# Expert blocks of two sizes, the last ones behind a branch

## The chip, the cores and the metric

One core of one Trainium2 chip runs the whole program. The metric is the device time of an execution in microseconds. Five engines work side by side, each through its own list of instructions: TensorE (PE in the profile, with its weight loads apart as PEld), VectorE (DVE), ScalarE (ACT), GpSimd (POOL) and SyncE (SP), which here only issues transfers. PE writes to PSUM; DVE and ACT copy from there to SBUF.

## What is computed

A sliding-window attention over 8 batches of 576 tokens with 8 heads of 64, and then a mixture of 8 experts. A token goes through one expert: the one of its own largest logit, or the one of the token before it.

```python
logits = np.einsum('bsd,de->bse', x, w_gate)                # x: attention's output, D = 512
local_gate = 1.0 / (1.0 + np.exp(-np.einsum('bsd,de->bse', x, w_local).squeeze(-1)))
for b in range(B):
    prev_e = -1
    for s in range(S):
        fresh_e = int(np.argmax(logits[b, s]))
        if s == 0 or local_gate[b, s] < 0.5:
            e = fresh_e
        else:
            e = prev_e if prev_e >= 0 else fresh_e
        prev_e = e
        ...                                                  # p: softmax of logits[b, s]
        h = np.maximum(x[b, s] @ w1[e], 0.0)                 # w1[e]: 512 x 1024
        out[b, s] = p[e] * (h @ w2[e])                       # w2[e]: 1024 x 512
```

All is float32. There are N = 4608 tokens.

## The kernel before

The program has three stages, each written as a function. A scheduler puts the instructions of each engine in order; it keeps their dependences and knows the buffers of each pool, and may pull an instruction ahead of others.

`attention` (lines 76 to 226) goes through 36 chunks of 128 tokens: scores (L127), a masked softmax (L137 to L149), the values' product (L177, L181), rows of x to DRAM (`xs`, L192), and the logits (L204).

`route` finds each token's expert and its place. Each expert's tokens take whole blocks of 256 places, so there are at most NBLK = 25 blocks, in NS = 50 slots of 128 places. `cnt` is the count of tokens of each expert, `ends` where its blocks end, `pl` and `plc` the place of each token, `ej` the expert of each block. A loop of 36 steps (L389 to L395) turns places around into `idx`, the token of each place, and `pw`, its gate's value. Places that stay empty hold the token N, whose row of `xs` is zero, and which the scatter leaves out.

`experts` runs a fixed number of blocks. For each, `fetch` reads the block's expert into a register of SP, gathers two slots of rows by indirect transfers on POOL (`xg`, L418), and loads that expert's `w1` and `w2`, 2 MB each, from SP's queue (L424). `turn` transposes the rows on PE (`tp`, L432; copied to `xt` by DVE). `hidden` is 8 groups of 4 matmuls into `hp` (L440) with 128 by 128 tiles of `w1` as weights and 256 columns of `xt` streaming; DVE and ACT take turns to evict with a relu (L443, L445). `result` runs, for each slot, 8 matmuls of 512 columns into `yp` (L452), an eviction scaled by the gate's value (L455), and an indirect scatter on POOL (L456). The loop fetches and turns a block ahead of the one it computes. Weights have two buffers for each of `w1` and `w2`, gathered rows four.

Of the kernel before, what the change touches and what calls it, by code (L numbers as in the profile page):

```python
# [8 lines left out]
F32 = mybir.dt.float32  # L9
I32 = mybir.dt.int32  # L10
# [8 lines left out]
P = 128  # L19
# [16 lines left out]
NS = NBLK * BC  # L36
NEG = -1.0e9


@with_exitstack  # L40
def kernel(
    ctx: ExitStack,
    tc: tile.TileContext,
    q: bass.AP,
    k: bass.AP,
    v: bass.AP,
    wg: bass.AP,
    w1: bass.AP,
    w2: bass.AP,
    out: bass.AP,  # L50
):
# [9 lines left out]
    ej = const.tile([1, NBLK], I32, name="ej")  # L61
# [12 lines left out]

@with_exitstack
def attention(ctx, tc, q, k, v, xs, lt, wgs, ident):
    """Softmax over the window for each chunk of 128 tokens, then its rows of x and its logits.

    q and k have two heads on the partitions. The keys of a chunk are its own and the 64 before it.
    Within a tile of four heads, slot 2 * j + i is head 4 * half + 2 * i + j.  # L80
    """
    nc = tc.nc
# [6 lines left out]

    # A query p of a chunk sees the keys p < j <= p + 64 of the 192.  # L90
    masks = []
# [61 lines left out]
    def values(st, half):  # L153
# [76 lines left out]
def route(ctx, tc, lt, idx, pw, ej, ident):  # L230
    """The expert of each token, and the tokens in order of their experts.

    Each expert's tokens take whole blocks of BLK places. Place 128 * n + p is at [p, n] in idx (the token)
    and pw (its gate's value); places that stay empty have the token N.
    """
    nc = tc.nc
# [116 lines left out]
    nb_i = tl("nb_i", P, E, dt=I32)  # L353
    nc.vector.tensor_scalar(nb_i, cnt, float(BLK - 1), None, Alu.add)
    nc.vector.tensor_scalar(nb_i, nb_i, BLK.bit_length() - 1, None, Alu.arith_shift_right)
    nb = tl("nb", P, E)
    nc.vector.tensor_copy(nb, nb_i)
    ends = tl("ends", P, E)
    nc.vector.tensor_tensor_scan(ends, nb, zero[:, :E], 0.0, Alu.add, Alu.add)
    off = tl("off", P, E)  # L360
    nc.vector.tensor_tensor(off, ends, nb, op=Alu.subtract)
    nc.vector.scalar_tensor_tensor(off, off, float(BLK), base[:, :, 0], Alu.mult, Alu.subtract)
    nc.vector.tensor_tensor(base, base, over(last(off), [P, E, C]), op=Alu.add)
    pl = tl("pl", *CE)
    nc.vector.tensor_tensor(pl, pre.rearrange("p (c e) -> p c e", e=E), base.rearrange("p e c -> p c e"), op=Alu.add)
    nc.vector.tensor_tensor(pl, pl, oh, op=Alu.mult)
# [11 lines left out]

    # The expert of block n: how many experts end at or before it.
    ec = tl("ec", 1, NBLK, E)  # L380
    nc.vector.tensor_tensor(ec, over(iob, [1, NBLK, E]),
                            over(ends[0:1, :].rearrange("p (o e) -> p o e", o=1), [1, NBLK, E]), op=Alu.is_ge)
    ef = tl("ef", 1, NBLK)
    nc.vector.tensor_reduce(ef, ec, axis=AX.X, op=Alu.add)
    nc.vector.tensor_scalar(ej, ef, float(E - 1), None, Alu.min)
# [15 lines left out]
def experts(ctx, tc, xs, w1, w2, out, idx, pw, ej, ident):  # L401
    """Each block's tokens through its expert: rows of x gathered, rows of the output scattered."""
    nc = tc.nc
    wp = ctx.enter_context(tc.tile_pool(name="ex_w", bufs=2))
    xp = ctx.enter_context(tc.tile_pool(name="ex_x", bufs=2 * BC))
    wk = ctx.enter_context(tc.tile_pool(name="ex_work", bufs=2))
    ps_t = ctx.enter_context(tc.tile_pool(name="ex_ps_t", bufs=2, space=PSUM))
    ps_h = ctx.enter_context(tc.tile_pool(name="ex_ps_h", bufs=3, space=PSUM))
    ps_y = ctx.enter_context(tc.tile_pool(name="ex_ps_y", bufs=2, space=PSUM))

    def fetch(n):
        st = {}
        e = nc.values_load(ej[0:1, n:n + 1], engines=[ET.SP], min_val=0, max_val=E - 1,
                           skip_runtime_bounds_check_because="a count of experts, at most E - 1")
        st["x"] = []
        for i in range(BC):
            x = xp.tile([P, D], F32, name="xg")
            nc.gpsimd.indirect_dma_start(  # L418
                out=x, out_offset=None, in_=xs[:, :],
                in_offset=bass.IndirectOffsetOnAxis(ap=idx[:, n * BC + i:n * BC + i + 1], axis=0))  # L420
            st["x"].append(x)
# [5 lines left out]
    def turn(st):  # L427
        st["xt"] = xt = wk.tile([P, DK, BLK], F32, name="xt")
        for i in range(BC):
            tp = ps_t.tile([P, DK, P], F32, name="tp")  # L430
            for kk in range(DK):
                nc.tensor.transpose(tp[:, kk, :], st["x"][i][:, kk * P:(kk + 1) * P], ident)  # L432
            nc.vector.tensor_copy(xt[:, :, i * P:(i + 1) * P], tp)

    def hidden(st):
        st["h"] = h = wk.tile([P, FK, BLK], F32, name="h")
        for m in range(FK):
            hp = ps_h.tile([P, BLK], F32, name="hp")
            for kk in range(DK):
                nc.tensor.matmul(hp, lhsT=st["w1"][:, kk, m * P:(m + 1) * P], rhs=st["xt"][:, kk, :],  # L440
                                 start=(kk == 0), stop=(kk == DK - 1))
            if m % 2:
                nc.vector.tensor_relu(h[:, m, :], hp)  # L443
            else:
                nc.scalar.activation(h[:, m, :], hp, Act.Relu)  # L445

    def result(st, n):
        for i in range(BC):
            s = n * BC + i
            yp = ps_y.tile([P, D], F32, name="yp")  # L450
            for m in range(FK):
# [6 lines left out]
                in_=y, in_offset=None, bounds_check=N - 1, oob_is_err=False)  # L458

    st = fetch(0)  # L460
    turn(st)
    for n in range(NBLK):
        nxt = fetch(n + 1) if n + 1 < NBLK else None
        hidden(st)
        if nxt:
            turn(nxt)
        result(st, n)
        st = nxt


# [29 lines left out]
```

## Time and profile before

| | |
|---|---|
| time, median of 3 runs | 1394.6 us (1388.53 to 1434.29) |
| span of the profiled execution | 1410.9 us (the profile has no other time of it) |
| PE busy | 1360.3 us, 96% |
| PEld busy | 1001.3 us, 71% |
| DVE, ACT, POOL busy | 332.0, 261.5, 134.5 us |
| first hidden layer starts | 694.80 us |
| DMA | 166.04 MB; q1 (SP's transfers) 133.17 MB, q0 (POOL's) 32.02 MB |

A row of the profile's groups names line, engine and operation, then what is written and read, the shape, the count, the busy time and the mean length of one in ns, and after the bar the idle time before them and what ended it. A row of the timeline starts with the start and the length of a merged run of instructions in us; PE's runs end with the last matmul's drain, so that neighbours overlap by some tenths. A row of the stretches has, after its bounds and length, the busy time (and number) of PE, PEld, DVE, ACT and POOL, then PE's granted clock, DMA's busy share and GB/s. Every float32 matmul leaves two records on PE and two on PEld; a transposition leaves one. The clock digits in the strip of slices are tenths of the full clock.

### The profile page before, as it was taken

What the parts mean: (1) busy time and instruction counts of PE and PEld (TensorE: products, weight loads), DVE (VectorE), ACT (ScalarE), POOL (GpSimd) and SP (SyncE); (2) the same over time, 40 slices, a digit from 0 to 9 for tenths busy, and PEclk for the clock granted to TensorE, in tenths of its full rate; (3) what the DMA queues carried; (4) which work ended last, traced back from release to release, by engine and by line L of the source; (5) the groups of instructions that cost most, each with busy time, mean ns of one, the idle gap of its engine ahead of it and who ended that gap; (6) DMA issues with size and microseconds to landing.
All of it is one profiled execution on the core that took longest, in us unless ns stands there. A gap on an engine that the chain in (4) does not pass through costs nothing. (4 is left out here: it accounts for less than half of the span.)

```text
span 1410.9 us, 13404 instructions
## 1 busy us (share of the span) xinstructions
PE 1360.3 (96%) x5322; PEld 1001.3 (71%) x5322; DVE 332.0 (24%) x688; ACT 261.5 (19%) x828; POOL 134.5 (10%) x222
## 2 busy tenths in 40 slices
PE   7999999999999999976499999999999999999998
PEld 5888788887888788865366677667766776667665
DVE  3533333233333334348110011001110011001100
ACT  3432332232232234220011111111101110111011
POOL 1000000000000000000201111111111111111100
PEclk7855555555555557555599999999999999999999
DMA  9202300033000000000745454545354545454520
GB/s 348 85 15 105 127 15 16 8 105 127 15 15 15 16 15 24 15 16 20 293 143 200 156 202 147 217 157 215 141 217 157 208 151 208 166 186 172 192 74 0
DMA packets 35678, 166.04 MB, mean 118 GB/s; under 512 B 4493, under 2 KB 16797, under 8 KB 29216
## 3 DMA queue, kind: packets, MB, share of 16 engines
q1 hardware_dynamic: 24672, 133.17, 25.8%
q0 software_dynamic: 10944, 32.02, 5.9%
q8 instruction: 42, 0.69, 0.2%
q14 instruction: 20, 0.16, 0.0%
HBM read 146.29 MB, written 22.55 MB: 120 GB/s over the span
## 5 line engine op out<-in xcount | busy, mean ns | idle before, releaser
L440 PE MATMUL hp<-xt,w 128*128 128x256 f32 x1600 | 352.0, 381 | 0.0
L452 PE MATMUL yp<-w,h 128*128 128x512 f32 x800 | 347.5, 592 | 0.0
L440 PEld LDWEIGHTS hp<-xt,w 128*128 128x128 f32 x1600 | 305.9, 191 | 52.2 <-issue 11.5
L452 PEld LDWEIGHTS yp<-w,h 128*128 128x128 f32 x800 | 150.3, 190 | 179.5 <-issue 179.4
L443 DVE TENSOR_SCALAR h<-hp 128x256 f32<-128x256 f32 x100 | 42.5, 425 | 631.0 <-issue 360.7
L127 PE MATMUL sp<-kt,qt 64*128 64x192 f32 (+1 forms) x576 | 179.6, 553 | 8.2 <-DMA kt<-in_k_dram 8.0
L177 PEld LDWEIGHTS xo<-vt,owns 128*128 128x128 f32 x576 | 120.7, 310 | 23.8 <-issue 21.3
L127 PEld LDWEIGHTS sp<-kt,qt 64*128 64x128 f32 x576 | 100.1, 297 | 50.7 <-issue 45.5
L149 ACT ACTIVATE e<-s,nmax 128x192 f32<-128x192 f32 (+1 forms) x288 | 125.5, 438 | 41.9 <-DVE nmax L141 41.4
L177 PE MATMUL xo<-vt,owns 128*128 128x64 f32 x576 | 131.3, 404 | 0.0
L181 PE MATMUL xo<-vt,befs 64*128 64x64 f32 x512 | 116.7, 402 | 0.0
L181 PEld LDWEIGHTS xo<-vt,befs 64*128 64x128 f32 x512 | 109.2, 309 | 7.0 <-issue 3.5
L455 ACT ACTIVATE y<-yp,pw 128x512 f32<-128x512 f32 x50 | 34.4, 687 | 380.2 <-PE yp L452 380.2
L445 ACT ACTIVATE h<-hp 128x256 f32<-128x256 f32 x100 | 38.3, 383 | 325.1 <-PE hp L440 325.1
L161 PE MATMUL own<-ident,e 128*128 128x128 f32 x288 | 90.7, 418 | 0.0
L137 DVE SCALAR_TENSOR_TENSOR s<-sp,mask 128x768 f32<-128x768 f32 x64 | 61.0, 954 | 124.4 <-PE sp L127 124.2
L170 ACT COPY befs<-bef 64x512 f32<-64x512 f32 x64 | 37.1, 580 | 275.0 <-PE bef L168 274.9
L456 POOL DMA_INDIRECT out_dram<-y,idx x50 | 50.4, 1009 | 366.2 <-ACT y L455 358.9
L163 DVE COPY owns<-own 128x512 f32<-128x512 f32 x72 | 49.7, 691 | 124.9 <-PE own L161 123.2
L418 POOL DMA_INDIRECT xg<-xs,idx x50 | 48.7, 973 | 318.2 <-PE tp L432 268.0
L168 PE MATMUL bef<-ident,e 128*128 128x128 f32 x256 | 75.7, 409 | 0.0
L161 PEld LDWEIGHTS own<-ident,e 128*128 128x128 f32 x288 | 54.5, 214 | 27.0 <-issue 17.0
(118 smaller groups left out, 647.6 us busy)
## 6 DMA issues: line engine op xcount, KB each, us to landing
w<-in_w_dram SPq DMA_DIRECT2D x50, 2048.0 KB, 8.8
qt<-in_q_dram SPq DMA_DIRECT2D x12, 768.0 KB, 9.1
kt<-in_k_dram SPq DMA_DIRECT2D x12, 768.0 KB, 10.5
vt<-in_v_dram SPq DMA_DIRECT2D x12, 768.0 KB, 11.6
xs<-x POOLq DMA_DIRECT2D x36, 256.0 KB, 2.3
xg<-xs,idx POOLq DMA_INDIRECT x50, 8.1
out_dram<-y,idx POOLq DMA_INDIRECT x50, 2.8
wgs<-in_wg_dram POOLq DMA_DIRECT2D x1, 18.0 KB, 4.5
```

The source lines that it names most:

```text
L127: nc.tensor.matmul(sp[:, j, i * KW + lo:(i + 1) * KW], lhsT=qt[h, 2 * half + i, t0:t0 + P], rhs=kt[h, 2 * half + i, t0 - WIN + lo:t0 + P], ...
L137: nc.vector.scalar_tensor_tensor(s.rearrange("p j i k -> p j (i k)"), sp[:, :, :2 * KW], DH ** -0.5, m.rearrange("p (o x) -> p o x", o=1). ...
L149: nc.scalar.activation(e[:, o + lo:o + KW], s[:, j, i, lo:], Act.Exp, bias=nmax[:, j, i:i + 1], accum_out=st["sum"][:, h:h + 1])
L161: nc.tensor.transpose(own[:, s, :], e[:, o:o + P], ident)
L163: nc.vector.tensor_copy(owns, own)
L168: nc.tensor.transpose(bef[:, s, :], e[:, s * KW:s * KW + P], ident)
L177: nc.tensor.matmul(st["xo"][:, head(s)], lhsT=owns[:, s, :], rhs=vt[:, c, head(s)], start=(half == 0 and s == 0), stop=bool(st["lo"]), ski ...
L181: nc.tensor.matmul(st["xo"][:, head(s)], lhsT=befs[WIN:, s, :], rhs=vt[WIN:, c - 1, head(s)], start=False, stop=True, skip_group_check=True)
L418: nc.gpsimd.indirect_dma_start(out=x, out_offset=None, in_=xs[:, :], in_offset=bass.IndirectOffsetOnAxis(ap=idx[:, n * BC + i:n * BC + i + ...
L440: nc.tensor.matmul(hp, lhsT=st["w1"][:, kk, m * P:(m + 1) * P], rhs=st["xt"][:, kk, :], start=(kk == 0), stop=(kk == DK - 1))
L452: nc.tensor.matmul(yp, lhsT=st["h"][:, m, i * P:(i + 1) * P], rhs=st["w2"][:, m, :], start=(m == 0), stop=(m == FK - 1))
L456: nc.gpsimd.indirect_dma_start(out=out[:, :], out_offset=bass.IndirectOffsetOnAxis(ap=idx[:, s:s + 1], axis=0), in_=y, in_offset=None, bou ...
```

## The change

An expert's tokens go first into complete blocks of 256, and what is left into blocks of 128. Of complete blocks there are at least NB = 11 whatever the counts are, and exactly the first 11, in the order of experts, are used; tokens beyond these, and all remainders, go to at most NSM = 21 blocks of 128. Eighteen of these (SURE) always run; the last three run only if more than 18 are in use. Their rows and weights are fetched ahead of the branch in either case. There are now 43 slots.

```diff
-BLK = 256
-BC = BLK // P
-NBLK = (N + E * (BLK - 1)) // BLK
-NS = NBLK * BC
+BIG = 2 * P
+NB = -(-(N - E * (BIG - 1)) // BIG)
+SM0 = NB * 2
+SMALL = N - NB * BIG
+NSM = (SMALL + E * (P - 1)) // P
+SURE = SMALL // P + E // 2
+NBLK = NB + NSM
+NS = SM0 + NSM
```

The places: `nb` is the number of an expert's big blocks after the cap at 11, `ns` of its small ones, `lim` the tokens in its big blocks, `rank` a token's number within its expert.

```diff
+    nc.vector.tensor_scalar(bend, bend, float(NB), None, Alu.min)
+    nc.vector.tensor_scalar(boff, boff, float(NB), None, Alu.min)
+    nc.vector.tensor_tensor(nb, bend, boff, op=Alu.subtract)
...
+    nc.vector.tensor_tensor_scan(send, ns, zero[:, :E], 0.0, Alu.add, Alu.add)
...
     pl = tl("pl", *CE)
-    nc.vector.tensor_tensor(pl, pre.rearrange("p (c e) -> p c e", e=E), base.rearrange("p e c -> p c e"), op=Alu.add)
+    nc.vector.tensor_tensor(pl, rank, over(mid(lim), CE), op=Alu.is_ge)
+    nc.vector.tensor_tensor(pl, pl, over(mid(step), CE), op=Alu.mult)
+    nc.vector.tensor_tensor(pl, pl, rank, op=Alu.add)
+    nc.vector.tensor_tensor(pl, pl, over(mid(off), CE), op=Alu.add)
     nc.vector.tensor_tensor(pl, pl, oh, op=Alu.mult)
...
+    nc.vector.tensor_copy(ej[:, NBLK:], send[0:1, E - 1:])
```

The expert stage: buffers, the hidden layer in groups of 512 columns of PSUM (two tiles of 256 or four of 128), and the branch.

```diff
-    wp = ctx.enter_context(tc.tile_pool(name="ex_w", bufs=2))
-    xp = ctx.enter_context(tc.tile_pool(name="ex_x", bufs=2 * BC))
+    wp = ctx.enter_context(tc.tile_pool(name="ex_w", bufs=4))
+    xp = ctx.enter_context(tc.tile_pool(name="ex_x", bufs=6))
...
-        for m in range(FK):
-            hp = ps_h.tile([P, BLK], F32, name="hp")
-            for kk in range(DK):
-                nc.tensor.matmul(hp, lhsT=st["w1"][:, kk, m * P:(m + 1) * P], rhs=st["xt"][:, kk, :],
-                                 start=(kk == 0), stop=(kk == DK - 1))
-            if m % 2:
-                nc.vector.tensor_relu(h[:, m, :], hp)
+        each = 512 // n
+        for g in range(FK // each):
+            hp = ps_h.tile([P, each, n], F32, name="hp")
+            for i in range(each):
+                m = g * each + i
+                for kk in range(DK):
+                    nc.tensor.matmul(hp[:, i, :], lhsT=st["w1"][:, kk, m * P:(m + 1) * P], rhs=st["xt"][:, kk, :n],
+                                     start=(kk == 0), stop=(kk == DK - 1))
+            o = h[:, g * each:(g + 1) * each, :n]
+            if g % 2:
+                nc.vector.tensor_relu(o, hp)
...
+    sure = NB + SURE
     st = fetch(0)
     turn(st)
-    for n in range(NBLK):
-        nxt = fetch(n + 1) if n + 1 < NBLK else None
+    for n in range(sure):
+        nxt = fetch(n + 1) if n + 1 < sure else None
...
+    rest = [fetch(n) for n in range(sure, NBLK)]
+    used = nc.values_load(ej[0:1, NBLK:NBLK + 1], min_val=0, max_val=NSM,
+                          skip_runtime_bounds_check_because="a count of blocks, at most NSM")
+    with tc.If(used > SURE):
+        for st in rest:
+            turn(st)
+            hidden(st)
+            result(st)
```

PE's list, at the end of the expert stage. Before, its last three blocks (`w_` tiles are buffers of `w1` under `hp` and of `w2` under `yp`):

```order
L440 MATMUL hp<-xt,w_6031 128x256 x32
L432 MATMUL tp<-ident,xg 128x128 x8
L452 MATMUL yp<-w_6033,h 128x512 x16
L440 MATMUL hp<-xt,w_6132 128x256 x32
L432 MATMUL tp<-ident,xg 128x128 x8
L452 MATMUL yp<-w_6134,h 128x512 x16
L440 MATMUL hp<-xt,w_6233 128x256 x32
L452 MATMUL yp<-w_6235,h 128x512 x16
L496 UNCONDITIONAL_BRANCH
```

The same place now, with the last two of the 18 small blocks that always run, and what stands behind the branch up to its first block:

```order
L487 MATMUL hp<-xt,w_5957 128x128 x32
L475 MATMUL tp<-ident,xg 128x128 x4
L499 MATMUL yp<-w_5959,h 128x512 x8
L487 MATMUL hp<-xt,w_6024 128x128 x32
L499 MATMUL yp<-w_6026,h 128x512 x8
L518 TENSOR_LOAD ej
L520 COMPARE_AND_BRANCH
L475 MATMUL tp<-ident,xg 128x128 x8
L487 MATMUL hp<-xt,w_6142 128x128 x32
L499 MATMUL yp<-w_6144,h 128x512 x8
```

A small block keeps the 32 matmuls of the hidden layer, with half the columns, and has half the transpositions and half the result matmuls of a big one; the next block's transpositions still stand between hidden layer and result.

DVE's list in `route`, between the count of tokens `cnt` and the sum `plc`, where PE has nothing to do. Before:

```order
L352 TENSOR_TENSOR cnt<-run,base 128x8
L354 TENSOR_SCALAR nb_i<-cnt 128x8
L355 TENSOR_SCALAR nb_i<-nb_i 128x8
L357 CAST nb<-nb_i 128x8
L359 SCALAR_TENSOR_TENSOR ends<-nb,zero 128x8
L361 TENSOR_TENSOR off<-ends,nb 128x8
L381 TENSOR_TENSOR ec<-iob,ends 1x200
L362 SCALAR_TENSOR_TENSOR off<-off,base 128x8
L384 TENSOR_REDUCE ef<-ec 1x25
L363 TENSOR_TENSOR base<-base,off 128x288
L385 TENSOR_SCALAR ej<-ef 1x25
L365 TENSOR_TENSOR pl<-pre,base 128x288
```

Now, the part of it from the small blocks' ends (`send`) on:

```order
L382 SCALAR_TENSOR_TENSOR send<-ns,zero 128x8
L384 TENSOR_TENSOR soff<-send,ns 128x8
L421 TENSOR_TENSOR ec<-iob,send 1x168
L389 SCALAR_TENSOR_TENSOR step<-soff,off 128x8
L426 CAST ej<-send 1x1
L424 TENSOR_REDUCE ef<-ec 1x32
L390 SCALAR_TENSOR_TENSOR step<-step,lim 128x8
L402 TENSOR_TENSOR pl<-pl,step 128x288
L425 TENSOR_SCALAR ej<-ef 1x32
L403 TENSOR_TENSOR pl<-pl,rank 128x288
L404 TENSOR_TENSOR pl<-pl,off 128x288
L405 TENSOR_TENSOR pl<-pl,oh 128x288
```

Counted over the whole stretch, instructions of 128x8 go from 7 to 20, and element-wise ones of 128x288 from 3 to 7; those for the blocks' experts (`ec`, `ef`, `ej`) are interleaved with the chain in both.

POOL's list at the start of the expert stage, as a piece of the difference: gathers (`xg`) and scatters (`out_dram`).

```order
+L461 DMA xg<-xs,idx 128x512 x12
+L503 DMA out_dram<-y,idx 4608x512 x4
+L461 DMA xg<-xs,idx 128x512 x2
+L503 DMA out_dram<-y,idx 4608x512 x2
+L461 DMA xg<-xs,idx 128x512 x2
```

Before, ten gathers stand in the place of the twelve, and the rest of this piece is the same; in the small blocks one gather alternates with one scatter. The attention's part of every engine's list is unchanged.

More of the change, by code (lines that the diff above doesn't have):

```diff
@@ L60 @@
     pw = const.tile([P, NS], F32, name="pw")
-    ej = const.tile([1, NBLK], I32, name="ej")
+    ej = const.tile([1, NBLK + 1], I32, name="ej")
     ident = const.tile([P, P], F32, name="ident")
@@ L353, in route @@
     nb_i = tl("nb_i", P, E, dt=I32)
-    nc.vector.tensor_scalar(nb_i, cnt, float(BLK - 1), None, Alu.add)
-    nc.vector.tensor_scalar(nb_i, nb_i, BLK.bit_length() - 1, None, Alu.arith_shift_right)
+    nc.vector.tensor_copy(nb_i, cnt)
+    nc.vector.tensor_scalar(nb_i, nb_i, BIG.bit_length() - 1, None, Alu.arith_shift_right)
     nb = tl("nb", P, E)
     nc.vector.tensor_copy(nb, nb_i)
-    ends = tl("ends", P, E)
-    nc.vector.tensor_tensor_scan(ends, nb, zero[:, :E], 0.0, Alu.add, Alu.add)
@@ L360, in route @@
-    off = tl("off", P, E)
-    nc.vector.tensor_tensor(off, ends, nb, op=Alu.subtract)
-    nc.vector.scalar_tensor_tensor(off, off, float(BLK), base[:, :, 0], Alu.mult, Alu.subtract)
-    nc.vector.tensor_tensor(base, base, over(last(off), [P, E, C]), op=Alu.add)
+    bend = tl("bend", P, E)
+    nc.vector.tensor_tensor_scan(bend, nb, zero[:, :E], 0.0, Alu.add, Alu.add)
+    boff = tl("boff", P, E)
+    nc.vector.tensor_tensor(boff, bend, nb, op=Alu.subtract)
+    nc.vector.tensor_scalar(bend, bend, float(NB), None, Alu.min)
@@ new lines, in route @@
+    nc.vector.tensor_scalar(boff, boff, float(NB), None, Alu.min)
+    nc.vector.tensor_tensor(nb, bend, boff, op=Alu.subtract)
+    lim = tl("lim", P, E)
+    nc.vector.tensor_scalar(lim, nb, float(BIG), None, Alu.mult)
+    rest = tl("rest", P, E)
+    nc.vector.scalar_tensor_tensor(rest, lim, -1.0, cnt, Alu.mult, Alu.add)
+    ns_i = tl("ns_i", P, E, dt=I32)
+    nc.vector.tensor_scalar(ns_i, rest, float(P - 1), None, Alu.add)
+    nc.vector.tensor_scalar(ns_i, ns_i, P.bit_length() - 1, None, Alu.arith_shift_right)
@@ L364, in route, with mid @@
+    first = tl("first", P, E)
+    nc.vector.tensor_copy(first, base[:, :, 0])
+    nc.vector.tensor_tensor(base, base, over(last(first), [P, E, C]), op=Alu.subtract)
+    rank = tl("rank", *CE)
+    nc.vector.tensor_tensor(rank, pre.rearrange("p (c e) -> p c e", e=E), base.rearrange("p e c -> p c e"), op=Alu.add)
+    def mid(ap):
+        return ap.rearrange("p (o e) -> p o e", o=1)
     pl = tl("pl", *CE)
-    nc.vector.tensor_tensor(pl, pre.rearrange("p (c e) -> p c e", e=E), base.rearrange("p e c -> p c e"), op=Alu.add)
+    nc.vector.tensor_tensor(pl, rank, over(mid(lim), CE), op=Alu.is_ge)
@@ L380, in route @@
     ec = tl("ec", 1, NBLK, E)
-    nc.vector.tensor_tensor(ec, over(iob, [1, NBLK, E]),
-                            over(ends[0:1, :].rearrange("p (o e) -> p o e", o=1), [1, NBLK, E]), op=Alu.is_ge)
+    for io, a, b, end in ((iob, 0, NB, bend), (iob, NB, NBLK, send)):
+        nc.vector.tensor_tensor(ec[:, a:b], over(io[:, :b - a], [1, b - a, E]),
+                                over(end[0:1, :].rearrange("p (o e) -> p o e", o=1), [1, b - a, E]), op=Alu.is_ge)
     ef = tl("ef", 1, NBLK)
     nc.vector.tensor_reduce(ef, ec, axis=AX.X, op=Alu.add)
-    nc.vector.tensor_scalar(ej, ef, float(E - 1), None, Alu.min)
+    nc.vector.tensor_scalar(ej[:, :NBLK], ef, float(E - 1), None, Alu.min)
+    nc.vector.tensor_copy(ej[:, NBLK:], send[0:1, E - 1:])
     tab = ps.tile([P, 2, NS], F32, name="tab", tag="e")
@@ L409, in experts, with slots @@
     ps_y = ctx.enter_context(tc.tile_pool(name="ex_ps_y", bufs=2, space=PSUM))
+    def slots(n):
+        return range(2 * n, 2 * n + 2) if n < NB else range(SM0 + n - NB, SM0 + n - NB + 1)
     def fetch(n):
-        st = {}
+        st = dict(x=[], slots=slots(n))
         e = nc.values_load(ej[0:1, n:n + 1], engines=[ET.SP], min_val=0, max_val=E - 1,
                            skip_runtime_bounds_check_because="a count of experts, at most E - 1")
-        st["x"] = []
-        for i in range(BC):
+        for s in st["slots"]:
             x = xp.tile([P, D], F32, name="xg")
@@ L427, in turn, with result @@
     def turn(st):
[L428 to L429 removed]
+        st["xt"] = xt = wk.tile([P, DK, BIG], F32, name="xt")
+        for i, x in enumerate(st["x"]):
             tp = ps_t.tile([P, DK, P], F32, name="tp")
             for kk in range(DK):
[L432 removed]
+                nc.tensor.transpose(tp[:, kk, :], x[:, kk * P:(kk + 1) * P], ident)
             nc.vector.tensor_copy(xt[:, :, i * P:(i + 1) * P], tp)
     def hidden(st):
[L436 to L449 removed]
+        n = len(st["slots"]) * P
+        st["h"] = h = wk.tile([P, FK, BIG], F32, name="h")
+        each = 512 // n
[9 more added lines that the diff above has]
+                nc.vector.tensor_relu(o, hp)
+            else:
+                nc.scalar.activation(o, hp, Act.Relu)
+    def result(st):
+        for i, s in enumerate(st["slots"]):
             yp = ps_y.tile([P, D], F32, name="yp")
```

13 lines of the change are left out of this document (11 added, 2 removed).

## The prediction

> **What bounds the kernel now.** I read the busy shares first, then the strip of 40 slices, then busy time by stretch, and last TensorE's timeline over one block of the expert stage.
>
> ```profile
> span 1410.9 us, 13404 instructions
> PE 1360.3 (96%) x5322; PEld 1001.3 (71%) x5322; DVE 332.0 (24%) x688; ACT 261.5 (19%) x828; POOL 134.5 (10%) x222
> ...
> PEclk7855555555555557555599999999999999999999
> ```
>
> TensorE is busy for 96% of the span, and its granted clock is about half in the first half of the program. By stretch (busy us of PE, weight loads PEld, DVE, ACT, POOL; then clock, DMA share, GB/s):
>
> ```profile
> 60.00:500.00 440.00, 440.00 (x1810) 355.51 (x1808) 151.76 (x254) 128.30 (x464) 20.14 (x69) 0.52 0.14 48
> 640.00:694.00 54.00, 28.24 (x93) 21.70 (x94) 28.76 (x126) 0.00 (x0) 8.62 (x9) 0.50 0.49 195
> 694.00:1405.00 711.00, 711.00 (x2580) 476.65 (x2580) 72.03 (x146) 71.98 (x149) 89.50 (x90) 1.00 0.45 165
> ```
>
> From 694 to 1405 lies the expert stage: PE without a gap, clock 1.00, DMA at 0.45, the other engines at 13% or less. So a PE instruction taken out there is worth its full time. One block of 256 tokens on PE, and the first and last rows of the stage:
>
> ```profile
> 694.80 16.53 PE L440 MATMUL hp<-xt,w 128*128 128x256 f32 x64
> 711.17 13.90 PE L452 MATMUL yp<-w,h 128*128 128x512 f32 x32
> ...
> 780.87 13.98 PE L440 MATMUL hp<-xt,w 128*128 128x256 f32 x64
> 794.68 1.04 PE L432 MATMUL tp<-ident,xg 128*128 128x128 f32 x8
> 795.55 13.90 PE L452 MATMUL yp<-w,h 128*128 128x512 f32 x32
> 809.29 13.98 PE L440 MATMUL hp<-xt,w 128*128 128x256 f32 x64
> ...
> 1391.55 13.90 PE L452 MATMUL yp<-w,h 128*128 128x512 f32 x32
> ```
>
> From start to start: hidden 794.68 - 780.87 = 13.81 us, or 0.216 us for each of 64 records (every f32 matmul leaves two); turning two slots 0.87; result 809.29 - 795.55 = 13.74, or 6.87 a slot. A block takes 28.42 us, whether its rows are tokens or padding.
>
> **The change: PE's work.** The stage goes from 25 blocks to 11 of 256 tokens and 18 of 128; three more stand behind a branch. Fourteen big blocks go: 14 x 28.42 = 397.9 us. A small block has half a block's result, 6.87, and half its turning, 0.44. Its hidden layer is the disputed term: it still has 32 matmuls and 64 records, since w1 needs the same 32 weight tiles, but each streams 128 columns instead of 256. By columns alone a record would take 0.216 / 2 = 0.108 us; but a weight load stands in each pair, and lasts longer than that:
>
> ```profile
> L440 PEld LDWEIGHTS hp<-xt,w x1600: 189/190/337, 694.6 to 1391.1; 128*128 128x128 f32 x178
> ...
> 7.99 1.81 PEld L127 LDWEIGHTS sp<-kt,qt 64*128 64x128 f32 x16 [7.99 <-issue]
> 8.02 2.08 PE L127 MATMUL sp<-kt,qt 64*128 64x128 f32 x16 [8.02 <-DMA kt<-in_k_dram]
> ...
> 45.01 0.97 PEld L177 LDWEIGHTS xo<-vt,owns 128*128 128x128 f32 x8 [0.23 <-issue]
> 45.01 1.10 PE L177 MATMUL xo<-vt,owns 128*128 128x64 f32 x8
> ...
> L177 PEld LDWEIGHTS xo<-vt,owns 128*128 128x128 f32 x8 | 1.0, 191 | 0.2 <-issue 0.2
> ...
> 8.02:10.20 2.18, 2.08 (x16) 1.78 (x16) 0.82 (x3) 0.00 (x0) 0.00 (x0) 1.00 1.05 380
> 45.00:48.00 3.00, 3.00 (x26) 2.85 (x25) 0.00 (x0) 1.88 (x9) 0.00 (x0) 1.00 0.01 3
> ```
>
> The 190 ns are a load's length, not its pace. At clock 1.00 the attention runs two streams that tell the pace: 16 pairs with 128 moving columns, whose loads fill 1.81 us, so (1.81 - 0.19) / 15 = 0.108 a pair; and eight pairs with a full 128 by 128 weight tile, (0.97 - 0.19) / 7 = 0.111. Loads overlap one another. The second has the small block's weights, the first its columns; I take 0.111, and keep 0.108 below and 0.190 (loads that don't overlap) above. Hidden is then 64 x 0.111 = 7.10, a small block 7.10 + 0.44 + 6.87 = 14.41, eighteen of them 259.4 us. PE's sum: -397.9 + 259.4 = **-138.5 us**.
>
> A rule speaks against that. The Trainium skill, "TensorE: Matmul & The Clock Gate", section on packing small matmuls, says that a weight load overlaps a running matmul only if the two use different row groups of the array. Here all pairs use all rows, so by it load and stream would add up; the trace disagrees at 256 columns, where a pair takes 0.216 us, its stream alone, not 0.111 + 0.216.
>
> **Branch and padding.** The reference's inputs give the experts 777, 371, 1129, 421, 433, 222, 530 and 725 tokens. In order of experts the first eleven complete blocks go 3, 1, 4, 1, 1, 0, 1, 0; what is left takes 1, 1, 1, 2, 2, 2, 3, 6 blocks of 128, which is 18 in all. `used > SURE` is false, the three blocks are jumped over, and only their 12.6 MB of weights and their gathers are still fetched.
>
> **Routing.** This runs on DVE with PE idle, so it counts in full.
>
> ```profile
> 638.73 0.17 DVE L354 TENSOR_SCALAR nb_i<-cnt 128x8 int32<-128x8 f32 x1
> 638.94 0.17 DVE L355 TENSOR_SCALAR nb_i<-nb_i 128x8 int32<-128x8 int32 x1
> ...
> 641.45 0.46 DVE L366 TENSOR_TENSOR pl<-pl,oh 128x288 f32<-128x288 f32 x1
> 641.95 0.45 DVE L369 TENSOR_REDUCE plc<-pl 128x36 f32<-128x288 f32 x1
> ```
>
> Thirteen more instructions of 128x8 at 0.21 us from start to start make 2.7, four more of 128x288 at 0.50 make 2.0, two more on one row about 0.4: +5 us if each waits for the one before, +3 if, as the scheduled order interleaves them, half of the short ones fall into others' latency. The narrower table (43 for 50 columns) saves a few tenths. I take **+5**.
>
> **Start of the experts.** Eight weight loads instead of four are issued at once, as the weight buffers go from 2 to 4, and six gathers instead of four.
>
> ```profile
> 675.95 1.08 PE L432 MATMUL tp<-ident,xg 128*128 128x128 f32 x4 [9.31 <-DMA xg<-xs,idx]
> ...
> 693.92 1.09 PE L432 MATMUL tp<-ident,xg 128*128 128x128 f32 x4 [2.65 <-DMA xg<-xs,idx]
> ...
> 684.00:688.00 4.00, 1.33 (x6) 0.71 (x4) 0.69 (x1) 0.00 (x0) 0.94 (x1) 0.50 1.04 433
> ```
>
> Six slots are turned before the first hidden layer, in both kernels, and their gathers land 3.6 us apart ((693.92 - 675.95) / 5) while weights fill the DMA (share 1.04, 433 GB/s). The longer backlog sits behind the first weights and leaves this rate as it is. I take 0; from -3 (gathers five and six issued earlier) to +4 (one more gather interval).
>
> **Transfers in the small blocks.** Cost nothing, if DMA keeps up.
>
> ```profile
> 780.87:809.29 28.42, 28.42 (x105) 19.07 (x104) 2.99 (x6) 2.91 (x6) 3.98 (x4) 1.00 0.48 177
> ...
> w<-in_w_dram SPq DMA_DIRECT2D x50, 2048.0 KB, 8.8
> ```
>
> A big block uses 0.48 x 28.42 = 13.6 us of DMA; its 4.19 MB of weights (two loads of 2048 KB) at 433 GB/s are 9.7 of that, its two gathers and two scatters 3.9. A small block has all the weights and half the rest: 11.7 us in 14.41, a share of 0.81. It fits, with 2.7 us to spare. Even if the two loads of 8.8 us ran one after the other (17.6 us), four weight buffers hide most: the first fifteen of the 29 blocks are loaded or under way when the first small block starts, the other fourteen take 14 x 17.6 + 7 = 253 us, and the last small block begins after 17 x 14.41 = 245. So 0, at most +8. SP queues only weight loads behind a waiting load; POOL alternates one gather and one scatter, about 2 us in 14.41.
>
> **Evictions** become half as many and twice as wide, and are hidden:
>
> ```profile
> L433 DVE COPY xt<-tp 128x512 f32<-128x512 f32 x50 | 32.4, 687 | 19.4 <-PE tp L432 19.1
> L455 ACT ACTIVATE y<-yp,pw 128x512 f32<-128x512 f32 x50 | 34.4, 687 | 380.2 <-PE yp L452 380.2
> ```
>
> By these rows a 128x512 eviction takes 0.69 us, while PE fills a buffer in 32 x 0.111 = 3.6 and has three. The last one of a block is wanted four result matmuls in, 3.4 us later. Without that cover it would cost about 0.7 us a block, 20 in all.
>
> **Tail.** The last rows now are
>
> ```profile
> 1405.54 0.69 ACT L455 ACTIVATE y<-yp,pw 128x512 f32<-128x512 f32 x1 [6.18 <-PE yp L452]
> 1406.50 0.98 POOL L456 DMA_INDIRECT out_dram<-y,idx  x1 [5.88 <-ACT y L455]
> ...
> L413 SPq TENSOR_LOAD <-ej x25: 262/269/473, 640.9 to 1321.5; - x25
> ```
>
> Each engine adds a register load (0.27 us) and a jump; only POOL's stands behind the last scatter, with SP's and PE's covered by the 5.4 us from PE's end (about 1405.5) to the span's. No row shows a jump over instructions. From 0 (hidden by the scatter's landing) to +3 (the whole 3.4 us after that scatter's issue spent again); I take +1, near the register load. The Trainium skill, "Runtime: NRT & Kernel Launch", on instruction fetch, warns that a taken branch whose target isn't prefetched waits for a fetch; no run here shows one.
>
> **Sum.** -138.5 + 5 + 0 + 0 + 1 = -132.5. The profiled execution gives a span, 1410.9, and no other time; it lies 1.2% above the median of the runs and inside their spread (1388.5 to 1434.3). I take the spread to come from the stretch at half clock, which the change leaves alone, and carry the difference over: a span of about 1278, and 1394.6 - 132 = **1263 us** for the median.
>
> **Rivals.**
> 1. *The clock falls in the small blocks* (slower). In 60 to 500 PE was busy throughout, loads filled 0.81 of it, and the clock was 0.52. A small block's hidden layer is loads from end to end. At half clock it takes 14.2 instead of 7.1, and the clock comes back late: the first row of the stage took 16.37 instead of 13.81, so another 2.6 in the result. 18 x 9.7 = 175 us: 1263 + 175 = 1438. It decides from a loss of 132 / 18 = 7.3 us a block. Against it: from 45 to 48 loads fill 2.85 of 3.00 us at clock 1.00, and the attention's streams are short (64 columns in 0.111 us), while here columns flow almost without pause. Chance 0.05.
> 2. *Loads don't hide.* At 0.190 a pair the hidden layer takes 12.2 and the gain is 397.9 - 18 x 19.5 - 6 = 41 (6 for routing and tail): 1354. That is against both attention streams; 0.03. If load and stream add up, 0.111 + 0.108 = 0.219 a pair, a small block takes 21.3, the gain is 8 and the time 1386; the 256-column pairs speak against it; 0.02. The Trainium skill's rule on row groups, above, would come to this.
> 3. *Weights bind.* +8 as worked out, 1271, or somewhat more if gathers wait behind weights as at the stage's start; 0.05. To cancel the gain the last fourteen loads would need (245 + 132 - 7) / 14 = 26 us each, 159 GB/s, below what a half-idle DMA moves now.
> 4. *The branch is taken*, through other roundings of the counts: three small blocks with little overlap, 3 x 14.41 + 8 = 51: 1314. An expert would need 13 tokens more; 0.02.
>
> **Chances and range.** The forecast has 0.83. Its ends: the fastest run and the low bounds, 1388.5 - 132 - 9 = 1247 (pace -3.5, start -3, routing -2); the slowest run, 1434.3 - 132 = 1302, which also holds the high bounds and rival 3 from the median or the profiled span. Faster by over 2% (about what a measurement of this kernel can tell from no change): 0.83 + 0.05 + 0.03 + 0.02 = 0.93, less a little for what I don't see, 0.92; within 2%: 0.03; slower: 0.05.
>
> **What would show it.** In the new trace: hidden rows of 128x128 taking 7.1 us a block with PE gapless and clock 1.00; blocks 28.4 and 14.4 us apart; DMA share near 0.8 late in the stage; about 5 us more from `cnt` to the first `rowh`; no PE work after the register load. A pace over 0.116, clock digits of 5 behind the big blocks, or PE waiting for `w` or `xg` would make it wrong.

## The result, and the profile after

| | before | after |
|---|---|---|
| time, median | 1414.4 us (4 runs, 1388.5 to 1434.3) | 1274.5 us (4 runs, 1266.5 to 1284.0) |
| span of the profiled execution | 1410.9 us | 1279.8 us |
| ratio of times | | 0.915, 95% interval 0.907 to 0.924 |

A later comparison with more runs (six against eleven) gave 0.911 (0.903 to 0.920; medians 1275.9 against 1401.1 us). The ratios leave out runs that lie more than 1.5% above the fastest of their kernel (the slow state), so they are not the quotients of the medians, which are of all runs. The prediction was 1263 us, with 1247 to 1302 as its range, and a span of about 1278.

The page's head and strip, and most of the stretch of small blocks as one row (columns as before), of the changed kernel:

```profile
span 1279.8 us, 13418 instructions
PE 1225.1 (96%) x5378; PEld 928.0 (73%) x5378; DVE 312.1 (24%) x637; ACT 240.4 (19%) x758; POOL 117.7 (9%) x205
...
PEclk7665555555555555665555999999999999999999
...
1010.00:1270.00 260.00, 260.00 (x1510) 190.96 (x1509) 22.59 (x35) 23.12 (x36) 32.03 (x33) 1.00 0.84 313
```

PE is as busy as it was, on less work. The last row, from 1010 to 1270 us, lies in the small blocks: PE without a gap in 260 us, clock 1.00, DMA share 0.84 where the big blocks of before had 0.48. PE's timeline, with the stage's first row, the first two small blocks and the last row:

```profile
702.00 16.39 PE L487 MATMUL hp<-xt,w 128*128 128x256 f32 x64
...
1014.88 7.31 PE L487 MATMUL hp<-xt,w 128*128 128x128 f32 x64
1022.02 0.60 PE L475 MATMUL tp<-ident,xg 128*128 128x128 f32 x4
1022.46 7.03 PE L499 MATMUL yp<-w,h 128*128 128x512 f32 x16
1029.33 7.31 PE L487 MATMUL hp<-xt,w 128*128 128x128 f32 x64
...
1267.67 7.03 PE L499 MATMUL yp<-w,h 128*128 128x512 f32 x16
```

A small block takes 1029.33 - 1014.88 = 14.45 us: hidden 7.14 (0.1116 a pair), turning 0.44, result 6.87. The stage lasts from 702.00 to 1274.70 (1267.67 + 7.03), 572.7 us; before it was 1391.55 + 13.90 - 694.80 = 710.65. The rest of the difference lies ahead of it: DVE's count `cnt` and the last step before the table's loop, first before, then after with SP's first weight load (before, that was issued at 666.84).

```profile
638.52 0.17 DVE L352 TENSOR_TENSOR cnt<-run,base 128x8 f32<-128x8 f32 x1
642.96 0.18 DVE L375 CAST lo<-lo_i 128x36 f32<-128x36 int32 x1
```

```profile
641.76 0.17 DVE L357 TENSOR_TENSOR cnt<-run,base 128x8 f32<-128x8 f32 x1
649.69 0.17 DVE L414 CAST lo<-lo_i 128x36 f32<-128x36 int32 x1
...
673.27 5.49 SPq L467 DMA_DIRECT2D w<-in_w_dram  x8
```

The account of the two spans, 1410.9 to 1279.8:

| stretch | before | after | difference | forecast |
|---|---|---|---|---|
| up to `cnt` (attention, first part of routing; unchanged) | 638.52 | 641.76 | +3.2 | 0 |
| `cnt` to `lo` | 4.44 | 7.93 | +3.5 | +5 |
| `lo` to the first weight load | 23.88 | 23.58 | -0.3 | a few tenths |
| first weight load to hidden(0) | 27.96 | 28.73 | +0.8 | 0 (-3 to +4) |
| expert stage | 710.65 | 572.70 | -138.0 | -138.5 |
| after PE's end | 5.45 | 5.10 | -0.4 | +1 |
| sum | 1410.9 | 1279.8 | -131.1 | -132.5 |

### The profile page after: what moved, and what is told of

It reads as the page before. It is cut to its first block, busy times and chain, and to the rows that moved or that the text cites. A ratio compares the mean times of both kernels' runs of the same rounds, so it can differ in the third digit from the quotient of the medians.

```text
span 1279.8 us, 13418 instructions
## 1 busy us (share of the span) xinstructions
PE 1225.1 (96%) x5378; PEld 928.0 (73%) x5378; DVE 312.1 (24%) x637; ACT 240.4 (19%) x758; POOL 117.7 (9%) x205
## 5 line engine op out<-in xcount | busy, mean ns | idle before, releaser
L487 PEld LDWEIGHTS hp<-xt,w 128*128 128x128 f32 x1856 | 267.0, 192 | 31.7 <-issue 13.4
L487 PE MATMUL hp<-xt,w 128*128 128x128 f32 (+1 forms) x1856 | 287.7, 316 | 0.0
L499 PE MATMUL yp<-w,h 128*128 128x512 f32 x640 | 279.5, 592 | 0.0
L499 PEld LDWEIGHTS yp<-w,h 128*128 128x128 f32 x640 | 119.5, 190 | 139.3 <-issue 137.0
L491 DVE TENSOR_SCALAR h<-hp 128x512 f32<-128x512 f32 x40 | 27.7, 692 | 523.0 <-issue 401.3
L502 ACT ACTIVATE y<-yp,pw 128x512 f32<-128x512 f32 x40 | 27.5, 687 | 367.6 <-PE yp L499 357.8
L503 POOL DMA_INDIRECT out_dram<-y,idx x40 | 40.1, 1003 | 308.1 <-ACT y L502 287.0
L145 DVE TENSOR_REDUCE nmax<-s 128x4 f32<-128x768 f32 (+1 forms) x72 | 66.1, 918 | 1.2
L493 ACT ACTIVATE h<-hp 128x512 f32<-128x512 f32 x40 | 23.9, 597 | 225.0 <-PE hp L487 225.0
```

The lines of the kernel that those rows point to most:

```text
L145: nc.vector.tensor_reduce(nmax, s[:, :, :, lo:], axis=AX.X, op=Alu.max, negate=True)
L487: nc.tensor.matmul(hp[:, i, :], lhsT=st["w1"][:, kk, m * P:(m + 1) * P], rhs=st["xt"][:, kk, :n], start=(kk == 0), stop=(kk == DK - 1))
L499: nc.tensor.matmul(yp, lhsT=st["h"][:, m, i * P:(i + 1) * P], rhs=st["w2"][:, m, :], start=(m == 0), stop=(m == FK - 1))
L503: nc.gpsimd.indirect_dma_start(out=out[:, :], out_offset=bass.IndirectOffsetOnAxis(ap=idx[:, s:s + 1], axis=0), in_=y, in_offset=None, bou ...
```

## Experiments

The theory: a block costs its time on PE, a small one 14.45 us because weight load and stream nearly balance at 128 columns; transfers, evictions and the branch are hidden. Against it stood, for each part, the rivals of the prediction. The stretch ahead of the stage differs between executions (the last point below), so the experiments are read by the stage: from hidden(0)'s start to the end of the last result.

**How much is the fewer rows alone?** The kernel before, cut to the 22 blocks in use.

```diff
-NBLK = (N + E * (BLK - 1)) // BLK
+NBLK = 22
```

> The kernel before, with its 25 blocks of 256 cut to the 22 that are in use for these inputs; nothing else changes. Theory (every block costs its 28.42 us on PE, padding or not): the expert stage shrinks by 3 x 28.42 = 85 us, from 710.7 to 625.4, and the time to about 0.94 of before. That would be 62% of the 138 us which the change took out of the stage; the other 53 us would be the small blocks' own. Rival (blocks of padding were cheap, since their scatter writes nothing and they gather one row again and again): a gain well under 85 us, and the small blocks did most of it.

First hidden and last result:

```profile
652.69 16.19 PE L440 MATMUL hp<-xt,w 128*128 128x256 f32 x64
...
1263.83 13.90 PE L452 MATMUL yp<-w,h 128*128 128x512 f32 x32
```

The stage is 1277.73 - 652.69 = 625.0 us, 85.6 less than before, where 85 was expected; the median time is 1324 us (four runs, 1284.9 to 1334.5) against 1405 (seven runs, six of them 1388.4 to 1413.8; one took 4961 us, and why is not known), 0.94 as expected, though with so wide a scatter the stage is the better evidence. Blocks of padding cost what full ones cost. Of the change's 138 us, 86 are what running exactly the blocks in use would bring (this cut holds for these counts alone), and 52 are the finer grain: 40 slots instead of 44.

**What sets a pair's pace, and does the clock hold?** Small blocks with 64, then 32 of their 128 columns in the hidden layer.

```diff
+            k = n if n == BIG else 64        # 32 in the second
-                    nc.tensor.matmul(hp[:, i, :], ..., rhs=st["xt"][:, kk, :n],
+                    nc.tensor.matmul(hp[:, i, :k], ..., rhs=st["xt"][:, kk, :k],
...
-                nc.tensor.matmul(yp, lhsT=st["h"][:, m, i * P:(i + 1) * P], rhs=st["w2"][:, m, :],
+                nc.tensor.matmul(yp[:k], lhsT=st["h"][:, m, i * P:i * P + k], rhs=st["w2"][:, m, :],
```

> The changed kernel, but a small block streams only 64 of its 128 columns through the hidden layer (the other 64 tokens of each small block are left out of hidden layer, result and scatter; the result matmuls still stream 512 columns). Theory (a pair lasts as long as the longer of weight load and stream, and at 128 columns the load's 0.111 us is the longer): hidden stays at 64 x 0.111 = 7.1 us and a small block at 14.45, clock 1.00. Rival one (the stream alone sets the pace): 64 x 0.056 = 3.6 us, a small block at 10.9, the stage 63 us shorter. Rival two (the clock goes by how much of the time columns stream, and 64 in 0.111 us is as thin as in the attention): clock 0.5 in the hidden layers, 14.2 us each and some in the result, a small block at up to 24, the stage up to 175 us longer.

> As with 64 columns, with 32 of the 128 columns of a small block streamed through the hidden layer (the other 96 tokens of each small block are left out). Theory (the weight load's pace binds): hidden 64 x 0.111 = 7.1 us still. Theory on the clock (it followed neither the load's share nor, at 64 columns, the share of streaming): 1.00 throughout; rival: with a quarter of the time streaming the clock falls to 0.5 in the hidden layers, 14.2 us each.

A block with 64 columns, and the stretches' row inside the hidden layer that follows it:

```profile
1225.75 7.36 PE L488 MATMUL hp<-xt,w 128*128 128x64 f32 x64
1232.94 0.60 PE L475 MATMUL tp<-ident,xg 128*128 128x128 f32 x4
1233.48 7.08 PE L501 MATMUL yp<-w,h 128*64 128x512 f32 x16
1240.49 7.36 PE L488 MATMUL hp<-xt,w 128*128 128x64 f32 x64
...
1240.00:1247.00 7.00, 7.00 (x60) 6.51 (x59) 0.00 (x0) 1.06 (x2) 0.90 (x1) 1.00 0.79 290
```

Half the columns save nothing: hidden takes 7.19 us (0.112 a pair), a block 14.74, the stage 576.3, and the clock stays at 1.00 (also over 982 to 1254.8 us, which holds all the small blocks). So a pair has a floor, and 128 columns stand right on it; a block of 64 tokens would cost as much as one of 128. That the floor is the weight load is the likeliest reading, as the loads' own pace read ahead of the change was 0.108 to 0.111 us; but no run changed the size of the load, so another cost that every pair has is not excluded. (The result even takes 7.01 us instead of 6.87 with weights of 64 columns; why was not tried.) With 32 columns, first a block and the whole stretch of small blocks, then four pieces of that block, two in its hidden layer and two in its result:

```profile
1013.90 9.94 PE L488 MATMUL hp<-xt,w 128*128 128x32 f32 x64
1023.65 1.09 PE L475 MATMUL tp<-ident,xg 128*128 128x128 f32 x4
1024.67 8.93 PE L501 MATMUL yp<-w,h 128*32 128x512 f32 x16
1033.54 9.16 PE L488 MATMUL hp<-xt,w 128*128 128x32 f32 x64
...
980.00:1345.00 365.00, 354.83 (x1554) 222.69 (x1552) 17.91 (x37) 18.55 (x38) 32.51 (x35) 0.78 0.60 223
...
1014.00:1018.00 4.00, 4.00 (x37) 4.00 (x37) 0.00 (x0) 0.95 (x2) 0.89 (x1) 1.00 0.76 250
1019.00:1023.00 4.00, 4.00 (x20) 4.00 (x21) 0.00 (x0) 0.00 (x0) 0.00 (x0) 0.50 0.40 164
1024.00:1028.00 4.00, 4.00 (x8) 1.06 (x7) 0.92 (x2) 0.00 (x0) 1.00 (x1) 0.50 0.80 274
1029.00:1033.00 4.00, 4.00 (x10) 0.99 (x9) 0.00 (x0) 0.00 (x0) 0.00 (x0) 1.00 0.49 205
```

Here the prediction's first rival comes true in part: the mean clock over the stretch is 0.78, hidden takes 9 to 10 us, the result 8 to 9 instead of 6.87, a block up to 19.6 us (1033.54 - 1013.90), and the stage 653.0 us, 80 more than the changed kernel's. So a falling clock was a real danger, with its edge between 32 and 64 columns for this layer; my theory on the clock, which took it as unmoved throughout, was wrong at 32. The loss falls short of the rival's 14.2 us since the clock is full at the hidden layer's start, falls to 0.50 within it and comes back within the result. That the fall comes inside the hidden layer also clears the result's narrower weights (32 columns) of it. And the floor of a pair goes with the clock: with 32 columns there are 37 records in 4 us at 1.00 and 20 at 0.50, so it is not a time that the clock leaves alone.

**Do the weights bind?** Two weight buffers instead of four (without the branch, whose three blocks need the room); and the opposite, one big block and 38 small ones.

```diff
-    wp = ctx.enter_context(tc.tile_pool(name="ex_w", bufs=4))
+    wp = ctx.enter_context(tc.tile_pool(name="ex_w", bufs=2))
```

```diff
-NB = -(-(N - E * (BIG - 1)) // BIG)
+NB = 1
```

> The changed kernel without the branch and its three blocks, and with two weight buffers instead of four. Theory (a small block's weights take 8.5 us each to land and are asked for one block, 14.45 us, ahead): PE still waits for nothing, small blocks 14.45 us, stage 572 us; the four buffers buy nothing but the room for the branch's blocks. Rival (loads need the depth): small blocks longer, up to 17.6 us if the two loads of a block run one after the other, the stage up to 57 us longer, PE waiting for w.

> The changed kernel with one block of 256 and 38 blocks of 128 that always run (again exactly the number in use), so 40 slots as before but ten big blocks replaced by twenty small ones; weights go from 134 to 176 MB. Theory (a slot costs 14.45 us in a small block and 14.21 in a big one, as load and stream nearly balance at 128 columns): stage longer by 20 x 14.45 - 10 x 28.42 = 5 us, PE without gaps, DMA share 0.84 throughout. Rival (weights bind once the lead from the big blocks is gone): PE waits for w in the first small blocks or all along, stage longer by 20 us or more.

The stretch of small blocks, with two buffers:

```profile
990.00:1240.00 250.00, 250.00 (x1469) 184.95 (x1469) 21.91 (x34) 22.53 (x36) 28.83 (x29) 1.00 0.82 304
```

and with 38 small blocks:

```profile
720.00:1250.00 530.00, 530.00 (x3091) 390.34 (x3090) 45.80 (x71) 47.51 (x74) 68.58 (x69) 1.00 0.89 324
```

Neither makes PE wait for weights once. The stages are 571.9 us, as without the branch at four buffers (571.7, below), and 576.6, where 577.7 was expected from 572.7 + 5. Even a DMA share of 0.89 (0.84 was expected) for 530 us leaves PE gapless. The four buffers buy the branch's fetches, no speed.

**What does the branch cost?** Taken always; and not there at all.

```diff
-    with tc.If(used > SURE):
+    with tc.If(used > 0):
```

```diff
-    rest = [fetch(n) for n in range(sure, NBLK)]
-    used = nc.values_load(...)
-    with tc.If(used > SURE):
-        ...
```

> The changed kernel with the branch's condition set to used > 0, so that the three blocks behind it run; for these inputs they hold padding alone. Theory (inside the branch nothing overlaps across blocks but what stands there, turn, hidden, result): 3 x 14.45 = 43 us plus about 8 us of waits, the span 51 us longer than the changed kernel's stage would give. Rival one (PE flows as in the loop): 43 us. Rival two (entering the branch makes every engine wait for the others and for instructions): 60 us or more.

> The changed kernel without the branch, the three blocks behind it and their transfers (places for more than 18 small blocks are not computed; these inputs have none). Theory (the register loads and jumps hide behind the last scatter, and the 12.6 MB of extra weights behind PE): expert stage 572.7 us as in the changed kernel, tail after PE's end 5 us, difference within 1 us. Rival (the extra loads or the jump cost something): stage or tail shorter by 3 us or more.

Taken, around the jump (the first row is the last block ahead of it) and at the end:

```profile
1262.40 7.03 PE L499 MATMUL yp<-w,h 128*128 128x512 f32 x16
1269.27 1.04 PE L475 MATMUL tp<-ident,xg 128*128 128x128 f32 x8
1270.65 7.41 PE L487 MATMUL hp<-xt,w 128*128 128x128 f32 x64 [0.35 <-DVE xt L476]
...
1307.42 7.03 PE L499 MATMUL yp<-w,h 128*128 128x512 f32 x16
```

From result to the branch's first transposition there is 1269.27 - 1262.40 = 6.87 us, the result's own length: entering costs PE nothing. Inside it waits 1.1 us in all, for `xt`. The stage is 617.9 us, 45.2 more than with the jump; three blocks are 43.4. The forecast of 51 was too dark: rival one, with 43 us, was nearest, and the one with 60 us or more falls. Without the branch:

```profile
705.33 15.35 PE L487 MATMUL hp<-xt,w 128*128 128x256 f32 x64
...
1269.96 7.03 PE L499 MATMUL yp<-w,h 128*128 128x512 f32 x16
```

stage 571.7 us, tail 1282.0 - 1276.99 = 5.0. The 1.0 us to the changed kernel is in the first hidden layer (15.35 against 16.39), where the clock is still rising: in stretches of 2 us it goes from 0.50 to 1.00 some 5 us after hidden(0)'s start in the changed kernel and some 3 us after it here. So the jump, the register loads and 12.6 MB of unused weights cost a tenth of a microsecond at most.

**Do the evictions' widths matter?** Narrow ones again.

```diff
-        each = 512 // n
+        each = 256 // n
```

> The changed kernel with the hidden layer's evictions left 256 columns wide, as before the change (one tile of 256 or two of 128 in each PSUM buffer). Theory (evictions lie beside PE either way): small block 14.45 us, big block 28.42, stage 572.7 us, no wait of PE on DVE or ACT. Rival (a small block fills a narrow buffer in 32 x 0.111 / 2 = 1.8 us and waits for its eviction): small blocks longer by 0.5 us or more, the stage by 9 us.

```profile
724.37 14.89 PE L487 MATMUL hp<-xt,w 128*128 128x256 f32 x64
...
1079.09 7.31 PE L487 MATMUL hp<-xt,w 128*128 128x128 f32 x64
1086.23 0.60 PE L475 MATMUL tp<-ident,xg 128*128 128x128 f32 x4
1086.67 7.03 PE L499 MATMUL yp<-w,h 128*128 128x512 f32 x16
1093.54 7.31 PE L487 MATMUL hp<-xt,w 128*128 128x128 f32 x64
...
1288.53 7.03 PE L499 MATMUL yp<-w,h 128*128 128x512 f32 x16
```

Small block 14.45 us, stage 571.2: no difference. From hidden(0) to the last result PE waits for nothing.

**What is left: the start.** The 28 us between the first weight load and hidden(0) are PE's longest idle time. A version gathers the rows of three blocks first and holds the second block's weights back until they are there. (In the code the store that waits stands behind the first block's `w1`; the scheduler issues that block's `w2` ahead of it too.)

```diff
+        if n == 0:
+            ahead.extend(rows(i) for i in range(3))
+        st["x"] = ahead[n] if n < 3 else rows(n)
         for name, w, a, b in (("w1", w1, DK, F), ("w2", w2, FK, D)):
...
+            if n == 0 and name == "w1":
+                nc.sync.dma_start(out=gate[0:1, :], in_=ahead[2][1][0:1, :16])
```

> The changed kernel, with the rows of the first three blocks gathered before anything else and the weights of the second and later blocks held back, by a 64-byte store that waits for the sixth gather, until these rows are there. Theory (the first six gathers are slow because eight weight loads share the DMA with them): with two loads in front of them, 5.8 MB at about 415 GB/s, they land within 14 to 18 us of the routing table instead of 28; hidden(0) starts 10 to 14 us earlier, counted from the first gather's issue, the rest of the stage stays at 572.7 us, and the time is about 12 us less than the changed kernel's. Rival (gathers come 3.5 us apart whatever else the DMA does): no change.

> The changed kernel again, beside the next one on one chip. Theory: as before, about 0.91 of the time before, with runs spread by 20 us or more, since the stretch ahead of the experts is 630 to 710 us long by how long the clock happens to be full in it, while the expert stage is always 572 us.

> The version with the first rows gathered ahead of the second block's weights, timed again beside the changed kernel. Theory: first gather's issue to hidden(0) 18 us instead of 28, so about 10 us less than the changed kernel, 0.8%, near 0.905 of the time before. Rival: the gain of the one look was chance, and both are the same.

The changed kernel's first and last transpositions ahead of hidden(0):

```profile
683.12 1.09 PE L475 MATMUL tp<-ident,xg 128*128 128x128 f32 x4 [10.06 <-DMA xg<-xs,idx]
...
701.12 1.09 PE L475 MATMUL tp<-ident,xg 128*128 128x128 f32 x4 [2.19 <-DMA xg<-xs,idx]
```

With the gate, timed beside the changed kernel (SP's loads and gate, then PE):

```profile
672.43 0.93 SPq L477 DMA_DIRECT2D w<-in_w_dram  x2
689.24 0.31 SPq L479 DMA_DIRECT2D gate<-xg  x1
...
681.91 1.09 PE L487 MATMUL tp<-ident,xg 128*128 128x128 f32 x4 [9.68 <-DMA xg<-xs,idx]
685.45 1.12 PE L487 MATMUL tp<-ident,xg 128*128 128x128 f32 x4 [2.46 <-DMA xg<-xs,idx]
687.34 3.54 PE L487 MATMUL tp<-ident,xg 128*128 128x128 f32 x16 [0.77 <-DVE xt L488]
690.72 13.98 PE L499 MATMUL hp<-xt,w 128*128 128x256 f32 x64
```

The first two gathers still come 3.5 us apart, beside the two loads; then the other four are there at once. POOL issues the six gathers at the same moments in both versions, from 0.97 to 7.34 us after the first weight load, so it is the weights held back that bring them sooner. Hidden(0) starts 690.72 - 672.43 = 18.3 us after the first load (19.4 in the first profile of this version) instead of 28.6 in the changed kernel on the same chip: about 10 us earlier, where 10 to 14 were expected at first. The stage is 570.3 us. The times: 0.899 (0.888 to 0.909) of before with the gate, from two runs only, and 0.911 (0.903 to 0.920) without. (A first series with the gate, on another chip, gave 1218.6 to 1270.1 us in four runs, against 1400.4 to 1419.6 before.) The intervals overlap; that the version is faster than the changed kernel rests on the 10 us of the profiles, and the medians of 1268.2 and 1275.9 us don't contradict it. It is faster than the kernel before beyond doubt.

## Why the prediction was right

- **What bounds it.** PE in the expert stage: the forecast was -138.5 us, the stage gave -138.0.
- **The disputed term.** The pace of 0.111 us read from eight pairs in the attention was 0.1116 in the small blocks, 7.14 us a layer instead of 7.10. The 190 ns of a single load would have given 12.2. The experiment with 64 columns shows that a pair has a floor of 0.112 us whatever streams; that the load is this floor fits its pace but is argued. The Trainium skill's sentence on row groups ("TensorE: Matmul & The Clock Gate", packing small matmuls) does not hold for these pairs, which all use the same rows: if load and stream added up, 128 columns would take 0.111 + 0.108 = 0.219 us, not 0.1116; the other case that its section names, a load into a background weight buffer, fits the time, but no row shows that buffer.
- **Padding and branch.** 18 small blocks ran and the three were jumped over; the cut to 22 blocks shows that padding is paid in full, so counting slots was the right measure. (Rival 4 is off by one: the 115 tokens left of one expert fill their block with 13 more, so a nineteenth block takes 14.)
- **Routing.** +5 forecast, +3.5 measured: nearer the lower case (+3), in which interleaving hides half of the short instructions. From `cnt` to `lo`, independent short instructions start 0.06 to 0.13 us after the one before, and those that need its outcome about 0.2.
- **Start.** +0.8 for 0: the doubled load queue left the gathers' pace as it was, as argued: 3.6 us ((701.12 - 683.12) / 5), as before. The experiment with the gate shows that the weights set it.
- **Transfers.** A share of 0.84 for the 0.81 expected, and no wait. The rival that weights bind falls with two buffers and with 38 small blocks.
- **Tail.** -0.4 for +1: the register load and the jump hide behind the last scatter but for 0.1 us (5.1 with them, 5.0 without). The rest of the difference to before comes without the branch too; its cause is open.
- **The clock.** It held, but the rival's danger exists: the clock fell at 32 columns. Its reason was wrong, though: loads from end to end don't bring the clock down by themselves, since they fill the layer with 64 columns as well. The change, at 128, has twice the columns of the layer that still kept the clock.
- **The time.** The span came out 1.8 us above the forecast. The median was 11 us above, and that is within the scatter of the medians: the one of before that I carried the gain to, 1394.6 of three runs, is 1414.4 with a fourth and 1401.1 in the longest series, and the difference to the changed kernel is 140 us in the first comparison and 125 in the second, with the forecast of 132 between them. That spread goes with the clock, as I took it to: in the eleven runs of before in the later comparison, the time rises from 1384.2 to 1419.9 us as the mean clock falls from 0.791 to 0.768. The traces below put it in the attention.

## What to carry to other kernels

When matmuls with the same weights get fewer columns, price the pair at the longer of its stream and its floor (here the load's pace, 0.111 us), and read the floor from start-to-start times of a stretch with short streams at full clock, not from one load's length: here both met at 128 float32 columns, and below that, fewer columns brought nothing, and at 32 they cost the clock. Count slots that run, padding included, before anything else; 86 of 138 us lay there. A runtime branch at a program's end, with its data fetched ahead, cost 0.1 us here, which makes it a cheap guard for work that is rarely needed.

## What the hardware showed that I had not expected

A busy PE doesn't keep the clock, and the number of columns has an edge. PE was busy throughout in the attention at half clock; hidden layers of small blocks kept the full clock with 128 and with 64 columns in 0.112 us, and lost it in block after block with 32. Between these layers little but the columns differs, so it is the columns that decide there. They don't account for the attention: between 60 and 500 us its 1810 records stream about 102 columns each (404 with 192 or 128, 746 with 64, 468 transpositions with 128, 192 with 9). By the 0.216 us that 256 columns take at full clock, this is, as an estimate, 0.68 of the time at a clock of 0.52, more than the 0.48 of the layers with 64 columns, which kept 1.00. What makes the difference, such as transpositions or the 750 records that use only 64 of the 128 rows, no run tried.

In the attention, which no experiment touches, the clock is at times full and mostly half, and differs between executions. The stretch 14 to 600 us of the kernel with narrow evictions, of the kernel before, of the changed one in the later comparison, and of the one with 22 blocks:

```profile
14.00:600.00 586.00, 586.00 (x2387) 474.12 (x2387) 198.77 (x333) 169.60 (x613) 26.39 (x92) 0.51 0.16 56
```

```profile
14.00:600.00 586.00, 586.00 (x2503) 474.37 (x2503) 208.44 (x349) 177.69 (x641) 27.90 (x97) 0.54 0.16 57
```

```profile
14.00:600.00 586.00, 586.00 (x2524) 474.33 (x2524) 209.45 (x351) 180.38 (x652) 27.91 (x97) 0.55 0.16 57
```

```profile
14.00:600.00 586.00, 573.56 (x2615) 465.66 (x2614) 226.94 (x413) 185.06 (x664) 30.27 (x106) 0.58 0.16 58
```

At clocks of 0.51, 0.54, 0.55 and 0.58 the first weight load was issued at 695.9, 666.8, 664.9 and 625.3 us. (Routing is 3.2 us longer in the first and third.) These 70 us, half the change's gain, are not the kernels' doing but for the 3 of routing: the attention's instructions are the same, and the first and the third, with the same routing and on one chip, lie 31 us apart. The expert stage meanwhile repeats within 2.4 us (570.3 to 572.7 in the seven profiles with 11 big and 18 small blocks that stream all their columns); a comparison of kernels like this is better read by the stage. What decides the clock in the attention was not tried.
